# Product 4 of the first weight pair goes to the second level; gates get near due times; some splits write three quarters of a tile

## The chip, the cores and the metric

The kernel runs on one core of a Trainium2 chip. The metric is the device time of one execution in microseconds. The engines are TensorE (PE, with its weight loads as PEld), VectorE (DVE), ScalarE (ACT), GpSimd (POOL) and SyncE (SP). SP and POOL issue nearly all DMAs here. Each engine works through its own instructions in the order in which the program lists them.

## The reference

All values are float32, with one batch of 2048 positions, a width of 512 and a hidden width of 1792.

```python
xn = _layernorm(x)                                        # x: 2048 x 512
a, b = xn @ dft_hid_re.T, xn @ dft_hid_im.T
y = dft_seq_re @ a - dft_seq_im @ b                       # 2048 x 512
h = gelu(xn @ w_gate) * (xn @ w_up)                       # 2048 x 1792
out = x + y + h @ w_down
```

## The kernel before

**Precision.** Each float32 operand of a matmul is split into a high part, which ACT rounds (`split_hi`), and a low part, which DVE makes as source minus high part (`split_lo`). A product of two such operands is three matmuls: high by high, high by low and low by high (`mm3`, line 305 issues them all).

**Seven products in place of eight.** Every matrix product is cut into 2 x 2 blocks and computed with seven block products after Strassen and Winograd, numbered 0 to 6. The sums of blocks that these need are made by DVE. In the feed-forward part a *unit* n is one column block of the gate and up weights for one half of the positions: units 0 to 13 (NP = 14) are the first half of the positions (`sp` 0), units 14 to 27 use the same weights on the second half (`sp` 1). Even units are gates, odd units are ups. A unit's product is six matmuls of 128 x 512.

**The second level.** For two of the seven products, 0 and 4, the product of a weight pair (units n and n+1, n even) with both halves of the positions is again a product of 2 x 2 blocks. Plainly it is four unit products (n, n+1, n+14, n+15) of six matmuls each, 24 in all. The second level makes it as seven inner products of three matmuls each, 21 in all. `LEAD[r]` is the first unit from which product r does so: `LEAD = {0: 0, 4: 2}` means from unit 0 for product 0, and from unit 2 for product 4. The inner products are called Xrk in the order strings (line 1727): X46 is inner product 6 of product 4. "Y43" in an odd unit's string is X43 of the pair that began a unit earlier. All seven run in the first half of the positions. What they yield for units n+14 and n+15 is written to DRAM (`park_m`, line 1606) and fetched back much later (`load_m`, line 1549), where ACT copies it into a PSUM bank as the start of that unit's sum (`seed`, line 1638).

What the inner products of product r need:

- sums of position blocks of both halves, `inner_x` (line 688, four of them, `xi` in the profile), each followed by a split on ACT and DVE. They may not begin before unit `LEAD[r] - INNER_AHEAD`, INNER_AHEAD being 2. For r = 4 they use the block sums that `sum_x` (line 1467, DVE line 1473) makes for the second half of the positions.
- sums of weight blocks of both units, `inner_w` (line 699, four instructions of 128 x 128 on DVE, `wi` in the profile), and one split.
- three ACT copies between PSUM banks or to SBUF (`copy`, line 1593) and two DVE additions (`sums`, line 1602).

The weights' own splits (`weight_split`, line 645) make two products' operands with one instruction on ACT and one on DVE: k = 0 makes those of products 0 and 1, k = 1 those of 4 and 5, each 128 x 512 elements (2 blocks of 256 columns). From units 14 on, where product 0 or 4 comes from the second level, only half of it is split (`half_split`).

**The planner.** The order of every instruction is made by `Plan` before the kernel is built. An operation has an engine, a cost, what it waits for, how many of the 109 SBUF tiles it takes (`SLOTS`), and a due time. `deadlines` (line 73) lays the PE operations end to end, gives each its start as due time, and works back from there to everything that feeds it. Operations that nothing waits for get a due time near the end of the plan; those that empty a PSUM bank get their matmul's end plus 4 us. `choose` (line 115) takes, engine by engine, what can start first, and keeps an operation that takes tiles from starting earlier than `early` us ahead of its due time, and a load from starting earlier than `ahead` us before its own. There are two plans: the first covers the layer norm, the plain part and half of the sequence DFT, up to about 200 us; the second covers the rest.

**The second plan's stages.** The sequence DFT goes on in 32 steps (`step_ops`, line 1024). A step loads panels of the DFT matrix, sums some (DVE), splits them (ACT and DVE), and multiplies. Sixteen steps make a chunk, in two halves of eight; between the halves DVE works through a chain of eight additions from PSUM (lines 1071 to 1081), and products of the second half wait for its end. Meanwhile `x_norm` (line 1397) normalizes the transposed input tile by tile: SP loads one of 16 tiles (`xr<-in_xt`), DVE subtracts and multiplies (lines 610 and 611), POOL stores it to DRAM (line 1405), and SP fetches it back for the feed-forward part (`xr<-xnt`, line 606). Then the hidden DFT products (`y`) and the units follow. The down products (`dn`) and the last `y` products are put into the gaps of the units' order strings (d0 to d3). `hidden` (line 1700) makes the gate (ACT) and its product with the up unit (DVE) out of PSUM banks.

Of the kernel before, what the change touches and what calls it, by code (L numbers as in the profile page):

```python
# [14 lines left out]
P = 128  # L15
# [24 lines left out]
class Plan:  # L40
# [15 lines left out]
    def done(self, name, at):  # L56
        self.ends[name] = at

    def add(self, name, engine, cost, fn, after=(), makes=(), uses=(), due=None, mb=0, banks=(), holds=(), adds=False, begin=0., ahead=None):
        assert name not in self.ops, name  # L60
        after = list(after)
        if engine == "p":
            if self.products:
                after.append(self.products)
            self.products = name
        self.ops[name] = dict(e=engine, cost=cost, fn=fn, after=after, makes=dict(makes), due=due, mb=mb, adds=adds, begin=begin, ahead=ahead or self.ahead, early=self.early, banks=tuple(banks), drains=bool(holds) and engine != "p")
        self.size.update(makes)
        for k in (*dict(makes), *uses):
            self.users.setdefault(k, set()).add(name)
        for k in (*banks, *holds):  # L70
            self.held.setdefault(k, set()).add(name)

    def deadlines(self):
        then = {n: [] for n in self.ops}
        for n, o in self.ops.items():
            for a in o["after"]:
                if a in self.ops:
                    then[a].append(n)
        t = self.clock["p"]
        for o in self.ops.values():  # L80
            if o["e"] == "p":
                o["due"], t = t, t + o["cost"]
        late = self.LATE if self.early == self.LATE else t - 1
        order, seen = [], set()

        def visit(n):
            stack = [(n, iter(then[n]))]
            seen.add(n)
            while stack:
                m, it = stack[-1]  # L90
                for c in it:
                    if c not in seen:
                        seen.add(c)
                        stack.append((c, iter(then[c])))
                        break
                else:
                    stack.pop()
                    order.append(m)
        for n in self.ops:
            if n not in seen:  # L100
                visit(n)
        for n in order:
            o = self.ops[n]
            own = late if o["due"] is None else o["due"]
            if o["due"] is None and o["drains"]:
                own = max([self.ops[a]["due"] + self.ops[a]["cost"] for a in o["after"] if a in self.ops and self.ops[a]["e"] == "p"],
                          default=late) + 4
            took = o["cost"] + (3.5 + o["mb"] * 2.6 if o["mb"] else 0)
            tail = self.TAIL[o["e"]]
            o["due"] = min([own] + [self.ops[c]["due"] - took - tail * (self.ops[c]["e"] != "p" or o["e"] != "p") for c in then[n]])  # L110
# [145 lines left out]
def fnet_geglu_kernel(ctx: ExitStack, tc: tile.TileContext, x, xt, cs, dh, wgu, wd, out):  # L256
# [34 lines left out]
    def split_lo(t, src, sign=1, engine=nc.vector):  # L291
        hi = t[0].bitcast(F32)
        if sign > 0:
            engine.tensor_sub(t[1], src, hi)  # L294
        else:
            engine.scalar_tensor_tensor(t[1], src, -1.0, hi, op0=OP.mult, op1=OP.subtract)
# [324 lines left out]
    wx, wl = {}, {}  # L621
# [7 lines left out]
    def weight_sums(n):  # L629
# [3 lines left out]
        def put(k, h, op, u, v):  # L633
# [3 lines left out]
            if (k, h) == (1, 1):  # L637
# [4 lines left out]
                lambda: put(1, 0, OP.subtract, a[:, 0], b[:, 1]),  # L642
                lambda: put(1, 1, OP.subtract, a[:, 1], r[0][:, 1]))

    def weight_split(n, k):

        if k == 0 and short(n):
            v = slot("wh", F32R, (P, 2, HD)), slot("wl", F32R, (P, 2, HD))
            wl[n, 1], wl[n, 3] = ((v[0][:, i], v[1][:, i]) for i in range(2))
            return v, wx[n][0]  # L650
        if half_split(n, k):
            p, src = {3: (3, wx[n][3][:, 0]), 0: (1, wx[n][0][:, 1]), 1: (5, wx[n][1][:, 1])}[k]
            wl[n, p] = hl_half("w")
            return wl[n, p], src
        v = slot("wh", F32R, (P, 2, HD)), slot("wl", F32R, (P, 2, HD))
        for r, p in enumerate(((0, 1), (4, 5), (6, 2))[k]):
            wl[n, p] = v[0][:, r], v[1][:, r]
        return v, wx[n][k]

    def load_wd(q):  # L660
# [3 lines left out]
            for i in range(2):  # L664
                nc.sync.dma_start(wx["d", q][i].rearrange("p a b -> p (a b)"), wd[q % (NP // 2), i])

    LEAD = {0: 0, 4: 2}
    LATER = {0: False, 4: False}
    KEEP_SUMS = (10, NP)

# [269 lines left out]
    for k in range(2, L):  # L940
        n, m = seq[k]
# [358 lines left out]


    HURRY = 28
    LOOSE = 15
    STEP_EARLY = 12, 16
    LATER_HURRY = 28
    FETCH_AHEAD = 22
    W_AHEAD = 12
    TURNS = [[0], [1, 2], [3, 4], [5, 6], [7, 8, 9], [10, 11], [12, 13]]
    INNER_AHEAD = 2
    INTO_ACC = (6, 3)  # L1310
    SUMS_AT = 0
    U1 = 2 * NP
    PARK = [(0, 0), (4, 0), *((k, i) for k in (1, 5, 2) for i in range(2))]

# [12 lines left out]
        plan.size[key] = size  # L1327
        plan.had.add(key)

    def split_of(key, f, ready, uses, makes, wide=True, due=None, **kw):  # L1330

        def hi():
            begun[key] = f()
            split_hi(*begun[key])
        add(("hi", key), "a", A5 if wide else A2, hi, after=ready, uses=uses, makes=makes, **kw)
        add(("lo", key), "v", V5 if wide else V2, lambda: split_lo(*begun.pop(key)), after=[("hi", key)], uses=[*uses, *makes], due=due)

    def unit_at(n):
        return TU + n * 14.25
# [52 lines left out]
    plan.early, plan.ahead = HURRY, FETCH_AHEAD  # L1392
    y_ops((4, 2, 6), "z")

    NORM_AT, NORM_STEP = 10, 8

    def x_norm(sp, t, d):
        n = (sp * 2 + t) * ND + d
        at = T2 + NORM_AT + NORM_STEP * n
        if d == 0:  # L1400
            add(("xst", sp, t), "s", .9, lambda: load_st(sp, t), makes={("xst", sp, t): 2}, mb=2 * MB)
        raw, key = ("nr", sp, t, d), ("xr", sp, d, t)
        add(("nl", sp, t, d), "s", .45, lambda: load_xr(sp, t, d, xt[sp, t, d]), makes={raw: 1}, mb=MB)
        add(("nn", sp, t, d), "v", 2 * V5, lambda: norm_xT(sp, t, d), after=[("nl", sp, t, d), ("xst", sp, t)], uses=[raw, ("xst", sp, t)], due=at)
        add(("np", sp, t, d), "g", .6, lambda: nc.gpsimd.dma_start(xnt[sp, t, d], xr[sp, d, t]), after=[("nn", sp, t, d)], uses=[raw], mb=MB, due=at + 4)
        add(("xl", sp, d, t), "s", .45, lambda: load_xr(sp, t, d, xnt[sp, t, d]), after=[("np", sp, t, d)], makes={key: 1}, mb=MB)

    for sp in range(2):
        for t in range(2):
# [3 lines left out]
    def units():  # L1413

        def weights(m):
# [23 lines left out]
            for k in range(3 if short(m) else 4):  # L1439
                half = half_split(m, k)  # L1440
                split_of(("w", m, k), lambda k=k: weight_split(m, k), [("sw", m, 3)],
                         [("ws", m, k - 1)] if k in (1, 2) else [("wx", m)], {("wl", m, k): 1 if half else 2}, not half)
        def park_sums(m, at, d):
            for i in range(2):
                nc.gpsimd.dma_start(ws_park[d, at, i], wx[m][1 + i].rearrange("p a b -> p (a b)"))
# [16 lines left out]
        for q in range(NP):  # L1462
            weights(("d", q))

        X_UNIT = {0: 0, 4: 1.5, 1: 3, 5: 8, 2: 9, 6: 12, 3: 12}

        def sum_x(sp, i, k):
            b11, b12, b21, b22 = (xr[sp, d, t] for d in (i, 2 + i) for t in range(2))
# [10 lines left out]
        def x_ops(sp, i):  # L1479
# [9 lines left out]
            for k, src, ready in ((0, x[0], load[0]), (1, x[2], load[2]), (2, x[3], load[3]), (4, x[1], ("sx", sp, i, 1)), (5, x[4], ("sx", sp, i, 2)),  # L1489
# [9 lines left out]
                if name[0] == "xp":  # L1499
                    add(("px", k, i), "g", 1.2, lambda k=k: park_xT(k, i), after=[("lo", ("x", 1, k, i))], uses=[name], mb=2 * MB, due=unit_at(X_UNIT[k] + i / 2 + 1.3))  # L1500
                    add(("fx", k, i), "s", .9, lambda k=k: fetch_one(k, i), after=[("px", k, i)], makes={("xt", 1, k, i): 2}, mb=2 * MB)

        for sp in range(2):
            for i in range(2):
                x_ops(sp, i)
# [11 lines left out]

        for r in LEAD:
            (o0, o1), (n0, n1) = ([("xr", sp, i, r // 4) for i in range(2)] for sp in range(2))
            made = [("sx", sp, i, 1) if r else ("xl", sp, i, 0) for i in range(2) for sp in range(2)]  # L1520
            for k, after, uses in ((4, [], [n0, o0]), (6, [], [n0, n1]), (5, [("ix", r, 4)], [n1, ("ix", r, 4)]),
                                   (3, [("ix", r, 5)], [o1, ("ix", r, 5)])):
                add(("ix", r, k), "v", V5, lambda r=r, k=k: inner_x(r, k), after=after + made, uses=uses, makes={("ix", r, k): 1},
                    begin=unit_at(LEAD[r] - INNER_AHEAD))
                split_of(("i", r, k), lambda r=r, k=k: inner_xsplit(r, k), [("ix", r, k)], [("ix", r, k)], {("ixt", r, k): 2},
                         begin=unit_at(LEAD[r] - INNER_AHEAD))

        def inner_ready(n, r, k):
            if k in (0, 1):
# [170 lines left out]
        def hidden(n, blk, ready, src, holds, uses):  # L1700

            q, s = n // 2, ("s", n // 2, blk)
            if n % 2 == 0:
                add(("f", n, blk), "a", A5, lambda: gate(n, blk, src()), after=ready, makes={s: 1}, holds=holds, uses=uses)
                return
            add(("f", n, blk), "v", V5, lambda: up_1(n, blk, src()), after=[*ready, ("f", n - 1, blk)], holds=holds, uses=[*uses, s])
            if blk in H_USE:
                r = H_USE[blk]
                add(("hi", ("h", q, r)), "a", A5, lambda: up_2(n, blk), after=[("f", n, blk)], uses=[s], makes={("hl", q, r): 2})
                add(("lo", ("h", q, r)), "v", V5, lambda: up_3(n, blk), after=[("hi", ("h", q, r))], uses=[s, ("hl", q, r)])  # L1710
# [209 lines left out]
```

## Time and profile before

| | |
|---|---|
| time, median of 3 runs | 788.95 us |
| the runs | 787.11, 788.95 and 789.32 us |
| the profiled execution's own time | 788.03 us |
| its span, first to last instruction | 786.2 us |

The profile comes from one further execution. Its span leaves out 1.8 us of that execution's time, which lies around the first and last instruction. The page lists busy time by engine, the chain of work that ended last, and groups of instructions by source line; views of the trace list single instructions with their starts, and busy time in stretches. PE's busy time overlaps from one matmul to the next, so for PE the distance between starts tells more than the busy share. The units run from 380.5 us on, and the last matmul starts at 782.6 us.

### The profile page before, as it was taken

To read this page: it belongs to the slowest core of one execution; us is meant where nothing else is said; L and a number is where in the kernel's file an instruction comes from. 1 tells how busy PE (TensorE), PEld (TensorE's weight loads), DVE (VectorE), ACT (ScalarE), POOL (GpSimd) and SP (SyncE) were. 2 spreads that over 40 slices of the span, in tenths; PEclk is the share of its full clock that TensorE was granted. 3 is DMA by queue.
4 is the path that set the end of the run, shared out by engine and by line. 5 is a ranking of instruction groups with operands and counts; after the bars stand their busy time and mean duration, and the time that the engine had idled before them with its cause. 6 is when DMAs were issued, how large, how long until landed. Compare 5 with 4: busy or idle time off the path is not lost.

```text
span 786.2 us, 11771 instructions
## 1 busy us (share of the span) xinstructions
PE 781.9 (99%) x3444; PEld 644.5 (82%) x3444; DVE 741.1 (94%) x1408; ACT 553.1 (70%) x1050; POOL 176.7 (22%) x266
## 2 busy tenths in 40 slices
PE   9999999999999999999999999999999999999998
PEld 6888888888887888888888888888888888888886
DVE  7999999999899699998999996999999989999986
ACT  6997555556545274556867876778797789788864
POOL 0120520043221041000122432343322112222200
PEclk9999999999999999999999999999999999999999
DMA  9966998779999879992745995797899975999942
GB/s 329 388 182 204 350 350 275 247 272 279 362 371 368 294 268 365 394 374 87 214 162 138 200 214 129 127 297 175 206 296 329 254 197 90 268 324 259 243 111 108
DMA packets 102928, 198.47 MB, mean 252 GB/s; under 512 B 12208, under 2 KB 21456, under 8 KB 102672
## 3 DMA queue, kind: packets, MB, share of 16 engines
q1 hardware_dynamic: 75312, 129.29, 47.1%
q0 software_dynamic: 27264, 68.17, 35.8%
q8 instruction: 27, 0.44, 0.2%
q14 instruction: 37, 0.30, 0.1%
q10 hardware_dynamic: 288, 0.26, 0.1%
HBM read 126.62 MB, written 74.20 MB: 255 GB/s over the span
## 4 chain that ended last, share of the span: by engine, by line
PE 99%; DMA 1%; DVE 0%; issue 0%
PE m L305 35%; PE b L305 20%; PE dn L305 17%; PE y L305 10%; PE c L305 8%; PE a L305 5%; PE z L305 4%; DMA xr<-in_xt 1%; PE warm L794 1%; DVE m L1081 0%; PE warm L796 0%; DVE p L1837 0%; PE st L1232 0%; DVE c L1079 0%
## 5 line engine op out<-in xcount | busy, mean ns | idle before, releaser
L289 ACT ACTIVATE psh<-pan 128x512 fp32r<-128x512 f32 x203 | 118.1, 626 | 77.5 <-DVE pan L581 26.2
L294 DVE TENSOR_TENSOR psl<-pan,psh 128x512 fp32r<-128x512 f32 x198 | 129.3, 685 | 0.1
L1686 POOL DMA_DIRECT2D partial<-part x80 | 70.0, 881 | 191.2 <-ACT part L1683 159.4
L305 PE MATMUL m<-psh,xch 128*128 128x512 f32 x232 | 90.4, 389 | 0.1
L305 PE MATMUL m<-psh,xcl 128*128 128x512 f32 x232 | 90.3, 389 | 0.0
L305 PE MATMUL m<-psl,xch 128*128 128x512 f32 x232 | 90.3, 389 | 0.0
L1683 ACT ACTIVATE part<-dn 128x512 f32<-128x512 f32 x80 | 47.1, 592 | 20.9 <-PE dn L305 16.7
L305 PEld LDWEIGHTS m<-psh,xch 128*128 128x128 f32 x232 | 43.5, 188 | 9.6 <-DVE m L1081 0.5
L305 PEld LDWEIGHTS m<-psl,xch 128*128 128x128 f32 x232 | 43.5, 188 | 9.0
L305 PEld LDWEIGHTS m<-psh,xcl 128*128 128x128 f32 x232 | 43.6, 188 | 9.0
L294 DVE TENSOR_TENSOR wl<-ws,wh 128x512 fp32r<-128x512 f32 x72 | 48.5, 685 | 1.6 <-ACT wh L289 1.6
L289 ACT ACTIVATE wh<-ws 128x512 fp32r<-128x512 f32 x72 | 43.6, 626 | 1.5 <-DMA partial<-part 1.2
L581 DVE TENSOR_TENSOR pan<-pan 128x512 f32<-128x512 f32 x58 | 39.1, 684 | 2.3 <-PE m L305 2.2
L305 PE MATMUL m<-psh,xa 128*128 128x512 f32 x116 | 40.4, 389 | 0.0
L546 POOL DMA_DIRECT2D partial<-part x28 | 20.8, 770 | 86.9 <-ACT part L542 73.2
L1046 POOL DMA_DIRECT2D t_park<-pan x29 | 16.5, 568 | 100.0 <-DVE pan L582 91.4
L289 ACT ACTIVATE hth<-s 128x512 fp32r<-128x512 f32 x56 | 34.1, 627 | 5.5 <-DVE s L753 5.3
L294 DVE TENSOR_TENSOR htl<-s,hth 128x512 fp32r<-128x512 f32 x56 | 37.3, 685 | 0.1
L753 DVE TENSOR_TENSOR s<-s 128x512 f32<-128x512 f32 x56 | 37.3, 685 | 0.1
L1599 ACT ACTIVATE q<-b 128x512 f32<-128x512 f32 x41 | 24.4, 596 | 14.4 <-PE b L305 14.1
L1599 ACT ACTIVATE w<-b 128x512 f32<-128x512 f32 x41 | 24.5, 597 | 13.9 <-PE b L305 11.2
L305 PE MATMUL dn<-htl,wh 128*128 128x512 f32 x84 | 32.7, 389 | 0.0
(760 smaller groups left out, 2419.4 us busy)
## 6 DMA issues: line engine op xcount, KB each, us to landing
pan<-in_cs SPq DMA_DIRECT2D x157, 256.0 KB, 6.5
partial<-part POOLq DMA_DIRECT2D x108, 256.0 KB, 5.2
wx<-in_wgu SPq DMA_DIRECT2D x48, 256.0 KB, 5.1
t_park<-pan POOLq DMA_DIRECT2D x29, 256.0 KB, 5.7
pan<-t_park SPq DMA_DIRECT2D x29, 256.0 KB, 6.0
wd<-in_wd SPq DMA_DIRECT2D x28, 256.0 KB, 5.5
acc<-partial SPq DMA_DIRECT2D x28, 256.0 KB, 4.7
m<-m_park SPq DMA_DIRECT2D x26, 256.0 KB, 6.0
```

Source lines behind the costliest of these rows:

```text
L289: nc.scalar.activation(t[0], src, AF.Copy, scale=float(sign))
L294: engine.tensor_sub(t[1], src, hi)
L305: nc.tensor.matmul(ps, a[u][:, sl], b[v], start=first and r == 0, stop=last and r == 2, skip_group_check=resumed)
L546: nc.gpsimd.dma_start(partial[sp, r, j], ypart.pop((r, j)), **({} if r in (0, 5, 6) else {"accum_op": OP.add}))
L581: return [lambda: nc.vector.tensor_sub(t3, b22, b12), lambda: nc.vector.tensor_sub(t1, b12, b11), lambda: (nc.vector.tensor_sub(b22, *((t1 ...
L753: nc.vector.tensor_sub(t, u, v)
L794: nc.tensor.matmul(ps, ones[:, :P], ones, start=i == 0, stop=False)
L1046: plan.add(("park", i), "g", .6, lambda: nc.gpsimd.dma_start(t2_park[c, k], pan_src[i][5]), after=[("S", i, 2)], mb=MB, uses=[("r", i, b22)])
L1599: nc.scalar.activation((bank if banks else side)[(n, to, *more)], src(), AF.Copy)
L1683: nc.scalar.activation(part[0], tiles[j], AF.Copy)
L1686: add(("da", qs[-1], r, j), "g", .6, lambda j=j, part=part: nc.gpsimd.dma_start(partial[sp, r, j], part[0], accum_op=OP.add), after=[("dc" ...
```

## The change

- `LEAD[4]` goes from 2 to 0, so that product 4 of units 0, 1, 14 and 15 is made by X40 to X46 in units 0 and 1. The order strings follow from it: unit 0 takes the first string below in place of the second, unit 1 the third in place of the fourth, and units 14 and 15 lose their product 4.
- `weight_split` leaves out the first 128 of the 512 columns in odd units of the first half of the positions where the product comes from the second level (`trimmed`): that quarter holds the half of product 0's (or 4's) operand that no inner product reads by itself (X03 and X43 read the other half). The planner's costs of these splits fall by 0.11 and 0.13 us.
- The planner gets `soon`: an operation that has it is due at the latest so many microseconds after it can be ready. Gates and their products with the up units have `SOON` = 5.
- Due times and limits move. Steps' tiles may be made 16 us ahead (12 before) and their loads 20 us ahead (16 before). The block sums and splits of the positions may be made 50 us ahead (28 before), and the normalized tiles fetched back 45 us ahead (22 before). Normalized tiles are due every 7 us (8 before). The second half's block sums begin one unit earlier, and its split for product 4 begins at unit 0.5 (1.5 before).

The order strings of `order`, lines 1729, 1731, 1733 and 1735, unchanged themselves:

```python
"X00 X40 d1 X01 X41 X04 5 1 X05 d2 6 X06 X44 d0 3 X03 X02 X45 2 d3 X46"    # lead(n, 4)
"X00 4 X01 d1 5 1 d2 X04 6 X05 d0 3 X06 d3 2 X03"                          # lead(n, 0) alone
"5 Y43 1 d1 Y42 d2 6 d0 3 d3 2"                                            # lead(n - 1, 4)
"4 Y02 d1 5 1 d2 6 d0 3 d3 2"                                              # lead(n - 1, 0) alone
```

```diff
     def deadlines(self):
...
+        ready = {}
+        for n in reversed(order):
+            o = self.ops[n]
+            ready[n] = o["due"] if o["e"] == "p" else max([ready[a] + self.ops[a]["cost"] for a in o["after"] if a in self.ops], default=0.)
         for n in order:
...
+            if o["soon"] is not None:
+                own = min(own, ready[n] + o["cost"] + o["soon"])
...
+    def trimmed(n, k):
+        return isinstance(n, int) and k < 2 and lead(n - 1, 4 * k)
+
     def weight_split(n, k):
...
+        if trimmed(n, k):
+            v, src = ([t.rearrange("p a b -> p (a b)")[:, P:] for t in u] for u in (v, (wx[n][k],)))
+            return v, src[0]
         return v, wx[n][k]
...
-    LEAD = {0: 0, 4: 2}
+    LEAD = {0: 0, 4: 0}
...
+    X_EARLY, X_FETCH = 50, 45
+    SOON = 5
     LOOSE = 15
-    STEP_EARLY = 12, 16
+    STEP_EARLY = 16, 20
...
-    SUMS_AT = 0
+    SUMS_AT = -1
...
-        add(("hi", key), "a", A5 if wide else A2, hi, after=ready, uses=uses, makes=makes, **kw)
-        add(("lo", key), "v", V5 if wide else V2, lambda: split_lo(*begun.pop(key)), after=[("hi", key)], uses=[*uses, *makes], due=due)
+        add(("hi", key), "a", (A5 if wide else A2) - .11 * less, hi, after=ready, uses=uses, makes=makes, **kw)
+        add(("lo", key), "v", (V5 if wide else V2) - .13 * less, lambda: split_lo(*begun.pop(key)), after=[("hi", key)], uses=[*uses, *makes], due=due)
...
-    NORM_AT, NORM_STEP = 10, 8
+    NORM_AT, NORM_STEP = 10, 7
...
-        add(("xl", sp, d, t), "s", .45, lambda: load_xr(sp, t, d, xnt[sp, t, d]), after=[("np", sp, t, d)], makes={key: 1}, mb=MB)
+        add(("xl", sp, d, t), "s", .45, lambda: load_xr(sp, t, d, xnt[sp, t, d]), after=[("np", sp, t, d)], makes={key: 1}, mb=MB, ahead=X_FETCH)
...
-        X_UNIT = {0: 0, 4: 1.5, 1: 3, 5: 8, 2: 9, 6: 12, 3: 12}
+        X_UNIT = {0: 0, 4: 0.5, 1: 3, 5: 8, 2: 9, 6: 12, 3: 12}
...
+        plan.early = X_EARLY
         for sp in range(2):
             for i in range(2):
                 x_ops(sp, i)
...
+        plan.early = HURRY
...
-                add(("f", n, blk), "a", A5, lambda: gate(n, blk, src()), after=ready, makes={s: 1}, holds=holds, uses=uses)
+                add(("f", n, blk), "a", A5, lambda: gate(n, blk, src()), after=ready, makes={s: 1}, holds=holds, uses=uses, soon=SOON)
                 return
-            add(("f", n, blk), "v", V5, lambda: up_1(n, blk, src()), after=[*ready, ("f", n - 1, blk)], holds=holds, uses=[*uses, s])
+            add(("f", n, blk), "v", V5, lambda: up_1(n, blk, src()), after=[*ready, ("f", n - 1, blk)], holds=holds, uses=[*uses, s], soon=SOON)
```

More of the change, by code (lines that the diff above doesn't have):

```diff
@@ L57, in done, with add @@
         self.ends[name] = at
-    def add(self, name, engine, cost, fn, after=(), makes=(), uses=(), due=None, mb=0, banks=(), holds=(), adds=False, begin=0., ahead=None):
+    def add(self, name, engine, cost, fn, after=(), makes=(), uses=(), due=None, mb=0, banks=(), holds=(), adds=False, begin=0., ahead=None, soon=None):
         assert name not in self.ops, name
@@ L65, in add @@
             self.products = name
-        self.ops[name] = dict(e=engine, cost=cost, fn=fn, after=after, makes=dict(makes), due=due, mb=mb, adds=adds, begin=begin, ahead=ahead or self.ahead, early=self.early, banks=tuple(banks), drains=bool(holds) and engine != "p")
+        self.ops[name] = dict(e=engine, cost=cost, fn=fn, after=after, makes=dict(makes), due=due, mb=mb, adds=adds, begin=begin, soon=soon, ahead=ahead or self.ahead, early=self.early, banks=tuple(banks), drains=bool(holds) and engine != "p")
         self.size.update(makes)
@@ L1328, in have, with split_of @@
         plan.had.add(key)
-    def split_of(key, f, ready, uses, makes, wide=True, due=None, **kw):
+    def split_of(key, f, ready, uses, makes, wide=True, due=None, less=False, **kw):
         def hi():
@@ L1441, in weights @@
                 split_of(("w", m, k), lambda k=k: weight_split(m, k), [("sw", m, 3)],
-                         [("ws", m, k - 1)] if k in (1, 2) else [("wx", m)], {("wl", m, k): 1 if half else 2}, not half)
+                         [("ws", m, k - 1)] if k in (1, 2) else [("wx", m)], {("wl", m, k): 1 if half else 2}, not half,
+                         less=trimmed(m, k))
         def park_sums(m, at, d):
```

## The prediction

> **What bounds the kernel now.** I read the page first: the span, the busy times, the clock row and the chain.
>
> ```profile
> span 786.2 us, 11771 instructions
> PE 781.9 (99%) x3444; PEld 644.5 (82%) x3444; DVE 741.1 (94%) x1408; ACT 553.1 (70%) x1050; POOL 176.7 (22%) x266
> PEclk9999999999999999999999999999999999999999
> PE 99%; DMA 1%; DVE 0%; issue 0%
> ```
>
> PE carries the chain at the full clock, and DVE has 6% to spare. A busy share can hide idle time, since matmuls overlap, so I went on to the chain in order of time and the starts of single matmuls.
>
> ```profile
> 96.98 76.16 PE m L305 x336
> ```
>
> These 336 matmuls in 76.16 us are one every 0.2267 us. That is the price of a matmul for as long as nothing keeps PE waiting. Going through all starts, I found three gaps that exceed it by over 0.15 us once the products have begun:
>
> ```profile
> 244.83 0.39 PE L305 MATMUL m<-psh,xf11l 128*128 128x512 f32 x1
> 245.29 0.50 PE L305 MATMUL m<-psh,xf11h 128*128 128x512 f32 x1
> ...
> 246.56 0.40 PE L305 MATMUL m<-psh,xf11l 128*128 128x512 f32 x1
> 247.05 0.49 PE L305 MATMUL m<-psh,xch 128*128 128x512 f32 x1
> ```
> ```profile
> 464.58 0.39 PE L305 MATMUL dn<-htl,w 128*128 128x512 f32 x1
> 464.98 0.50 PE L305 MATMUL b<-xT30h,w 128*128 128x512 f32 x1
> 465.31 0.39 PE L305 MATMUL b<-xT30l,w 128*128 128x512 f32 x1
> ```
>
> Each stall is the distance less 0.227, and the start after it is late too (0.33 for 0.227, as the last pair shows). The first two are 0.23 and 0.27 plus about 0.11 each, so 0.7 us; the third is 0.17 + 0.10, so 0.3 us. **All stalls together are about 1.0 us.** The kernel can be helped in two ways alone: fewer matmuls, or this 1.0 us. The Trainium skill, Perfetto Trace Analysis, Identifying the Most-Contended Engine, speaks against the first: it calls matmul busy time no good measure and takes the busy share of LDWEIGHTS. By that share, 82% on the page, TensorE has slack, and the sum would be 0 for the matmuls in place of the -0.68 below; the starts above do not bear that out.
>
> **The matmuls.** Product 4 of units 0, 1, 14 and 15 was 4 x 6 = 24 matmuls and becomes 7 x 3 = 21: three fewer, 3 x 0.2267 = **-0.68 us**. This is the only certain term. They move too: the first pair gets 21 - 12 = 9 more (+2.04 us), units 14 and 15 get 12 fewer (-2.72 us).
>
> **DVE, over the whole run.** Prices are distances between starts, since a busy DVE overlaps its instructions:
>
> ```profile
> 395.47 0.42 DVE L636 TENSOR_TENSOR ws<-wx 128x256 f32<-128x256 f32 x1
> 395.81 0.42 DVE L294 TENSOR_TENSOR w<-wx,w 128x256 fp32r<-128x256 f32 x1
> ...
> 402.76 0.28 DVE L707 TENSOR_TENSOR wi<-wi,wx 128x128 f32<-128x128 f32 x1
> 402.96 0.28 DVE L707 TENSOR_TENSOR wi<-wx 128x128 f32<-128x128 f32 x1
> ...
> 425.25 0.68 DVE L294 TENSOR_TENSOR xT41l<-xr,xT41h 128x512 fp32r<-128x512 f32 x1
> 425.86 0.68 DVE L294 TENSOR_TENSOR xi43l<-xi,xi43h 128x512 fp32r<-128x512 f32 x1
> ```
>
> 128 columns cost 0.20, 256 cost 0.34 and 512 cost 0.61 us. No row has 384 columns; the bounds are 0.34 and 0.61, and I take the middle, 0.47, because the three lie on a line. The new pair adds 4 x 0.20 (`inner_w`), one split and two `sums` at 0.61: 2.6 us. The half splits in units 14 and 15 save 2 x 0.27 and the 14 trimmed ones (seven odd units, k = 0 and 1) 14 x 0.14: 2.5 us. DVE's total stays. ACT gains three copies, a split and two seeds, six at about 17.12/35 = 0.5 us each (the stretch below, ACT's busy time over its count), and has 30% idle. Two stores on POOL and two loads on SP of 256 KB are added; POOL is 78% idle, and the seeds that wait for the loads are needed for product 2, late in a unit. I price all of this at nothing; if a seed's load came late, PE would stand for up to the 6.0 us such a load takes:
>
> ```profile
> m<-m_park SPq DMA_DIRECT2D x26, 256.0 KB, 6.0
> 580.00:600.00 20.00, 20.00 (x90) 16.53 (x89) 19.96 (x41) 17.12 (x35) 5.78 (x8) 1.00 1.04 335
> ```
>
> The DMA engines are full there (1.04, the number before the last), but 26 such loads already run from there on without a stall, each asked for up to 22 us ahead by the planner.
>
> **DVE, where it matters: units 0 and 1.** What product 4 needs is not new, it is early. This is PE's first matmul of unit 0:
>
> ```profile
> 380.46 0.39 PE L305 MATMUL a<-xT00h,wh 128*128 128x512 f32 x1
> ```
>
> In the new string X44 stands behind 45 matmuls (X00 3, X40 3, d1 6, X01, X41, X04 9, 5 and 1 12, X05 3, 6 6, X06 3), so it is due at 380.46 + 45 x 0.2267 = 390.7; X45 behind 66 at 395.4, X46 behind 75 at 397.5, X43 behind 84 at 399.5. Before, the same work stood here:
>
> ```profile
> 357.45 0.42 DVE L636 TENSOR_TENSOR ws<-ws,wx 128x256 f32<-128x256 f32 x1
> 361.62 1.33 DVE L1177 TENSOR_TENSOR zr<-c,zr 128x512 f32<-128x512 f32 x2 [3.75 <-ACT c L1145]
> ...
> 394.27 0.69 DVE L1603 TENSOR_TENSOR w<-c,w 128x512 f32<-128x512 f32 x1 [0.34 <-ACT w L1599]
> ...
> 397.42 0.69 DVE L1195 TENSOR_TENSOR zr<-zr 128x512 f32<-128x512 f32 x1
> ...
> 398.95 0.68 DVE L1603 TENSOR_TENSOR q<-c,q 128x512 f32<-128x512 f32 x1
> ...
> 408.08 0.69 DVE L1473 TENSOR_TENSOR t<-xr 128x512 f32<-128x512 f32 x1
> ...
> 412.56 0.69 DVE L693 TENSOR_TENSOR xi<-xr 128x512 f32<-128x512 f32 x1
> ```
>
> The four block sums of the second half (from 408.08), four `xi` sums (from 412.56) and their four low splits (the last at 425.86 above) are 12 x 0.61 = 7.3 us; with `inner_w` and its split, 1.4, **8.7 us must be in by 399.5** that were not. Cover: the idle 3.75 and 0.34 us in these rows, together 4.1; work of 395 to 399 that nobody needs yet (four 128x256 sums of unit 2's weights, two `zr`, a parked `q`: 4 x 0.34 + 3 x 0.61 = 3.2); two trimmed splits, 0.3. That is 7.6, and 1.1 us has to go earlier than 350. There is a hole for it:
>
> ```profile
> 260.00:270.00 10.00, 10.00 (x46) 8.29 (x45) 7.88 (x13) 3.15 (x7) 1.08 (x2) 1.00 0.96 328
> 270.00:280.00 10.00, 10.00 (x46) 8.29 (x45) 5.47 (x9) 5.86 (x12) 1.59 (x3) 1.00 0.48 185
> ...
> 330.00:340.00 10.00, 10.00 (x46) 8.28 (x45) 10.00 (x18) 5.57 (x11) 0.00 (x0) 1.00 1.05 388
> ...
> 350.00:360.00 10.00, 10.00 (x46) 8.29 (x45) 7.87 (x14) 6.21 (x11) 0.00 (x0) 1.00 0.37 138
> 360.00:370.00 10.00, 10.00 (x45) 8.28 (x45) 8.32 (x14) 6.24 (x11) 0.00 (x0) 1.00 0.33 107
> ```
>
> DVE (fourth number) leaves 2.1 + 4.5 us at 260 to 280. Steps' tiles may now be made 16 us ahead instead of 12, and the normalizing ends about 15 us sooner, so more than 1.1 us can slip back into it. I take the stall in unit 0 or 1 at zero, with bounds of -0.3 (the stall at 464.58 may go) and +4.9 (second rival).
>
> **Loads.** X44 needs the block sums by about 386, so four tiles fetched late must come sooner:
>
> ```profile
> xr<-xnt SPq DMA_DIRECT2D x16, 256.0 KB, 5.4
> SPq L556 <- PE m L305: 10.5, 2, 9.6
> ```
> ```profile
> 349.34 0.96 SPq L627 DMA_DIRECT2D wx<-in_wgu  x2
> 360.25 1.46 SPq L556 DMA_DIRECT2D zr<-z_park  x2
> ...
> 373.47 1.47 SPq L606 DMA_DIRECT2D xr<-xnt  x2
> ...
> 377.95 1.21 SPq L606 DMA_DIRECT2D xr<-xnt  x2
> ```
>
> Issued at 373 and 378 and landing 5.4 us later (first row), they would just do; with 45 us of allowance they go into SP's queue ahead of weights, `zr` and `dh`. SP stands still from 350 to 360, mostly until PE's last steps free tiles (9.6 us, second row), and the DMA share is 0.37 and 0.33 from 350 to 370: the four fit by bandwidth, if they find tiles. Normalizing closer together (7 for 8 us, from 208 on)
>
> ```profile
> L610 DVE TENSOR_TENSOR xr<-xr,bst x16: 682/685/694, 208.4 to 324.5; 128x512 f32<-128x512 f32 x16
> ```
>
> puts (250 - 208)/7 - (250 - 208)/8 = 0.75 tile more, two transfers of 256 KB each, in front of 250, where the engines are full (rival three).
>
> **Gates.** `soon` adds no instruction; it moves gates ahead of splits. ACT has idle time; on DVE, one up product put in front of an operand that is just in time costs at most 0.61 us once. I take zero.
>
> **The sum.** 788.03 - 0.68 = 787.35 us for an execution like the profiled one. The median of the runs is 0.92 above that execution, which gives 788.27 by it. I take a value between: **787.7 us**. A measurement of this kernel tells about 0.3%, 2.4 us, from no change, and the runs before spread over 2.2.
>
> **The rivals.**
>
> 1. *The stalls go as well.* The chain of additions at 245 gets a new order on DVE. For it: DVE gets ahead earlier. Against: it is as full there as before. 788.03 - 0.68 - 1.0 = 786.35 (787.3 by the median). Chance 0.2.
> 2. *Slower: DVE is late for X44 to X43.* The hole at 357 to 361 is a wait in DVE's queue, with SP short of tiles at the same time; if the second half's tiles find no room before the steps end at 364, neither this hole nor the one at 260 takes any of the 8.7 us. Then 8.7 - 0.34 - 3.2 - 0.3 = 4.9 us are missing, and PE stands behind X44 with every product of the unit queued after it: 788.03 - 0.68 + 4.9 = 792.2. It makes the kernel slower by over 0.3% once 3.1 us are missing. For it: DVE is at 10.00 of 10 from 330 on and PE's order is fixed. Against: units 2 and 3 ran the same strings before without a gap. Chance 0.11. The Trainium skill (Perfetto Trace Analysis, Per-engine timelines) says that ACT and DVE are strictly first in, first out; the 3.75 us row, with later work ready, agrees.
> 3. *A late load at 240 to 250.* 0.75 x 2 transfers of 256 KB at the 388 GB/s of a full stretch are 1.0 us, DVE waits in its queue, and the stall at 245 grows by it: 788.35 (789.3 by the median). Chance 0.16.
> 4. *PE has slack, so that the three matmuls were never paid for* (the change then moves no time): 788.03. The starts speak against it. Chance 0.03.
>
> **How the numbers follow.** The forecast keeps 0.5. Range: 785.9 (the first rival less half a microsecond of scatter) to 790.6 (the third by the median, with scatter, or half of the second); most of the second lies outside. Faster by over 0.3% means below 786.6 against the median: about half of the first rival and a little of the forecast's scatter, 0.14. Slower: the second and little else, 0.12. Within: 0.74.
>
> **What would show it.** The profile after should have 3441 matmuls, the same distance between starts, `xi44l` before 390.7, and no start of PE between 380 and 400 that is late. A gap of PE at X44 to X43 with DVE behind it is the second rival, a longer one near 245 the third. I am wrong by more than the range if the new order of the second plan stalls in a stage that I have priced at zero.

## The result, and the profile after

| | before | changed |
|---|---|---|
| time, median of 13 runs each, side by side | 788.82 us | 790.12 us |
| lowest and highest | 787.11, 789.36 | 789.31, 791.85 |
| profiled execution | 788.03 | 790.12 |
| its span | 786.2 | 788.3 |

The ratio is 1.0024, with a 95% interval of 1.0016 to 1.0032. The time lies inside the predicted range and within 0.3%, but on the other side: 1.1 us less were forecast, 1.3 us more came out.

From the page of the changed kernel, the span, the busy times, the granted clock and the chain by engine:

```profile
span 788.3 us, 11776 instructions
...
PE 780.9 (99%) x3441; PEld 643.8 (82%) x3441; DVE 743.2 (94%) x1415; ACT 555.5 (70%) x1056; POOL 177.6 (23%) x268
...
PEclk9999999999999999999999999999999999999999
...
PE 88%; issue 5%; DMA 2%; DVE 2%; POOL 2%; ACT 1%; POOLq 0%; DVEq 0%; ACTq 0%
```

The clock is full and three matmuls are gone, as meant; DVE's 94% is as before. What differs is the chain: PE carried 99% of it and carries 88% now. Other engines let PE wait somewhere, and the busy shares don't say where. So I listed every start of PE once more. This is PE's timeline of the changed kernel (start, duration, operation, and in brackets the idle time before it with what ended it) at each distance that is too long, and at two matmuls that the prediction named:

```profile
389.10 0.39 PE L311 MATMUL b<-xT61h,wl 128*128 128x512 f32 x1
389.70 0.50 PE L311 MATMUL b<-xi06h,wih 128*128 128x512 f32 x1 [0.21 <-ACT q L1617]
...
390.50 0.40 PE L311 MATMUL c<-xi44h,wih 128*128 128x512 f32 x1
...
399.35 0.39 PE L311 MATMUL b<-xi43h,wh 128*128 128x512 f32 x1
...
412.72 0.39 PE L311 MATMUL c<-xT41h,wl 128*128 128x512 f32 x1
414.04 0.50 PE L311 MATMUL c<-xi04h,wih 128*128 128x512 f32 x1 [0.93 <-DVE s L752]
...
467.82 0.39 PE L311 MATMUL dn<-htl,w 128*128 128x512 f32 x1
469.08 0.50 PE L311 MATMUL b<-xT30h,w 128*128 128x512 f32 x1 [0.88 <-ACT w L1617]
...
526.80 0.39 PE L311 MATMUL b<-xT51h,wl 128*128 128x512 f32 x1
527.38 0.50 PE L311 MATMUL b<-xi43h,wh 128*128 128x512 f32 x1 [0.20 <-ACT w L1617]
```

Less the usual 0.227, and with 0.11 each for the late start behind it, there are four stalls: **A** at 389 (0.48 us), **B** at 412 (1.20), **C** at 467 (1.15, where before lost 0.3) and **D** at 527 (0.47). The two near 245 are gone. The whole run, from the starts of the matmuls:

| us, profiled executions | before | changed | difference |
|---|---|---|---|
| first product starts | 5.25 | 5.41 | +0.16 |
| stalls (distances over 0.235, less 0.227 each) | 1.40 | 3.74 | +2.34 |
| all the rest up to the last matmul's start | 775.97 | 775.37 | -0.60 |
| last matmul starts | 782.62 | 784.52 | +1.90 |

The three matmuls brought their 0.6 to 0.7 us, and stalls took 2.3. None of them stands at X44 to X43, where the prediction had looked for one: X44 ran at 390.50 and X43 at 399.35, without a wait. But A, at X06 just ahead of X44, is a late start between 380 and 400, one of its signs, and C stands at the same pair of matmuls as the stall of 0.3 us at 464.58 that it had listed.

**Stall A.** First ACT's timeline of the changed kernel, with the places of C and D for later, then that of before, and from PE's timeline of before X06 and, for stall B, X04:

```profile
386.62 0.62 ACT L295 ACTIVATE xT01h<-xr 128x512 fp32r<-128x512 f32 x1
387.26 1.28 ACT L747 ACT_TABLE_LOAD   x1
388.56 0.60 ACT L747 ACTIVATE s<-a 128x512 f32<-128x512 f32 x1
389.05 0.59 ACT L1617 ACTIVATE q<-b 128x512 f32<-128x512 f32 x1
...
466.94 0.63 ACT L295 ACTIVATE hh<-s 128x512 fp32r<-128x512 f32 x1 [1.84 <-DVE s L752]
467.48 1.06 ACT L1701 ACTIVATE part<-dn 128x512 f32<-128x512 f32 x2
468.43 0.60 ACT L1617 ACTIVATE w<-b 128x512 f32<-128x512 f32 x1
...
526.73 0.60 ACT L1617 ACTIVATE w<-b 128x512 f32<-128x512 f32 x1 [0.45 <-DMA partial<-part]
```
```profile
386.72 1.28 ACT L735 ACT_TABLE_LOAD   x1
388.01 0.60 ACT L735 ACTIVATE s<-a 128x512 f32<-128x512 f32 x1
...
390.18 0.60 ACT L1599 ACTIVATE q<-b 128x512 f32<-128x512 f32 x1
```
```profile
392.70 0.39 PE L305 MATMUL b<-xi06h,wih 128*128 128x512 f32 x1
...
411.06 0.39 PE L305 MATMUL c<-xi04h,wih 128*128 128x512 f32 x1
```

X06 adds to the bank in which X05's sum stands, and the copy `q<-b` has to read that sum out first. X06 starts when this copy ends, at 389.64. That copy stands behind the first gate, and the first gate brings the load of the GELU table along, 1.28 us in which ACT does nothing else. In before the same load began 0.5 us sooner, at 386.72, but X06 came at 392.70, 1.9 us after its copy had ended (390.18 + 0.60). In the new string X06 is due at 389.33, 3.4 us sooner, and the load has become the thing that it waits for.

**Stall B.** DVE's timeline of the changed kernel, with rows for other steps, and that of before:

```profile
384.35 0.69 DVE L300 TENSOR_TENSOR xi44l<-xi,xi44h 128x512 fp32r<-128x512 f32 x1
...
389.50 0.56 DVE L300 TENSOR_TENSOR wl<-wx,wh 128x384 fp32r<-128x384 f32 x1
389.97 0.69 DVE L300 TENSOR_TENSOR xT01l<-xr,xT01h 128x512 fp32r<-128x512 f32 x1
...
397.30 0.69 DVE L300 TENSOR_TENSOR xi43l<-xi,xi43h 128x512 fp32r<-128x512 f32 x1
...
411.77 0.68 DVE L300 TENSOR_TENSOR z310l<-zr,z310h 128x512 fp32r<-128x512 f32 x1
412.37 0.68 DVE L300 TENSOR_TENSOR z311l<-zr,z311h 128x512 fp32r<-128x512 f32 x1
412.97 0.42 DVE L642 TENSOR_TENSOR ws<-ws,wx 128x256 f32<-128x256 f32 x1
413.31 0.68 DVE L752 TENSOR_TENSOR s<-s,b 128x512 f32<-128x512 f32 x1
...
460.87 0.43 DVE L642 TENSOR_TENSOR ws<-wd 128x256 f32<-128x256 f32 x1 [2.27 <-DMA wd<-in_wd]
```
```profile
406.54 0.69 DVE L294 TENSOR_TENSOR z310l<-zr,z310h 128x512 fp32r<-128x512 f32 x1
...
409.62 0.68 DVE L740 TENSOR_TENSOR s<-s,b 128x512 f32<-128x512 f32 x1
```

X04 of the second pair opens a PSUM bank that this up product (`s<-s,b`) has to leave first. In before the up product began at 409.62 and X04 ran at 411.06 without a wait. Now it begins at 413.31, behind two splits and a weight sum for later matmuls. It ends at 413.99, and PE starts at 414.04. The same three stood ahead of it in before, but there the first of them began at 406.54, 5.2 us sooner (411.77 now): DVE's queue as a whole comes later to this place, and PE's X04 only 1.9 us later.

**Stalls C and D.** At C DVE stands 2.27 us for a `wd` load (460.87), ACT then stands 1.84 us for DVE (466.94), and the copy `w<-b` that frees PE's bank follows only at 468.43, behind two copies of down products. At D the copy waits for a tile that a store still reads. These are chains of several engines; A and B each hang on the place of one instruction, as the runs below show.

### The profile page after: what moved, and what is told of

Read it like the earlier page. It is cut to its first block, busy times and chain, and to the rows that moved or that the text cites. A ratio compares the mean times of both kernels' runs of the same rounds, so it can differ in the third digit from the quotient of the medians.

```text
span 788.3 us, 11776 instructions
## 1 busy us (share of the span) xinstructions
PE 780.9 (99%) x3441; PEld 643.8 (82%) x3441; DVE 743.2 (94%) x1415; ACT 555.5 (70%) x1056; POOL 177.6 (23%) x268
## 4 chain that ended last, share of the span: by engine, by line
PE 88%; issue 5%; DMA 2%; DVE 2%; POOL 2%; ACT 1%; POOLq 0%; DVEq 0%; ACTq 0%
PE m L311 35%; PE b L311 15%; PE dn L311 15%; PE y L311 9%; PE c L311 5%; PE z L311 4%; PE a L311 4%; POOL partial L1704 1%; DMA partial<-part 1%; DMA wd<-in_wd 1%; POOL m_park L1625 0%; DMA x<-in_x 0%; DVE ws L642 0%; DVE wl L300 0%; POOL xT_hl L625 0%
## 5 line engine op out<-in xcount | busy, mean ns | idle before, releaser
L300 DVE TENSOR_TENSOR wl<-ws,wh 128x512 fp32r<-128x512 f32 (+1 forms) x70 | 46.4, 672 | 2.1 <-ACT wh L295 2.0
L295 ACT ACTIVATE wh<-ws 128x512 fp32r<-128x512 f32 (+1 forms) x70 | 42.4, 616 | 1.7 <-DVE ws L642 1.3
L311 PE MATMUL dn<-hth,wh 128*128 128x512 f32 x84 | 32.7, 389 | 0.0
```

The lines of the kernel that those rows point to most:

```text
L295: nc.scalar.activation(t[0], src, AF.Copy, scale=float(sign))
L311: nc.tensor.matmul(ps, a[u][:, sl], b[v], start=first and r == 0, stop=last and r == 2, skip_group_check=resumed)
```

## The experiments

The theory: stalls A and B come of two instructions that stand too late in the queues of ACT and DVE, and neither engine is short of time. The first rival: DVE is full, so an operation moved ahead there makes another one late. The second: the loss lies with the later stalls, whatever happens in units 0 to 3. All edits start from the changed kernel. "Stalls" are worked out from the profiled execution as in the table above; they are given with the late start behind them. Each group of runs has before in it, so kernels of different groups compare best by their ratios to before. The closer normalizing of the tiles and the earlier block sums were not undone singly.

**The changed kernel again**, no edit:

> The changed kernel once more, for a second trace. Two theories stand. Theory 'order': the 2.3 us that the stalls grew by come from single instructions that stand in the wrong place in an engine's order; then the stalls that follow from the order alone, 0.6 us at 389 and 1.3 us at 412.7, stand in this trace again to within 0.1 us, while those at 468 (1.3 us) and 527 (0.6 us), which followed a late transfer or a tile that came free late, may differ by up to 1 us. Time 790.1, give or take 0.6. Rival 'shortage': DVE has too much to do from 350 us on, so that the lost time moves about; the first two stalls shift by several us or change size.

790.48 us, ratio to before (788.49 in this group) 1.0026 [1.0017, 1.0035]. The stalls stood at 389.08, 412.70, 467.78 and 526.79, within 0.04 us of the first profile; A, B and C have the same size within 0.04 us, D is 0.70 for 0.47. They belong to the program, not to one execution.

**The table load earlier.** One GELU of a scratch column between the two plans, where ACT waits anyway:

```diff
     first_half = plan
+    nc.scalar.activation(junk[:, :1], eps, AF.Gelu_apprx_tanh)
```

> One gate function on 128x1 elements is added on ACT between the two plans, at about 200 us, so that the table load of 1.28 us, which stands at 387.3 us right ahead of the first gate, happens there. Theory 'order': the copy that X06 waits for is no longer behind the table load, and the stall at 389 (0.48 us and 0.11 us after it) goes; the stall at 412.7 stays at 1.3. Time 0.6 below the changed kernel, 789.5. Rival 'shortage': X06 finds its operands late from DVE as well, and the stall stays or moves to the next inner product; 790.1.

789.71 us, 1.0014 [1.0005, 1.0023]: 0.8 us below the changed kernel. ACT's timeline shows the load in its new place, and none follows up to the first gate:

```profile
201.77 1.28 ACT L1330 ACT_TABLE_LOAD   x1
203.06 0.21 ACT L1330 ACTIVATE junk<-eps 128x1 bf16<-128x1 f32 x1
```

Stall A is gone and B is unchanged (1.10 + 0.11 at 412.62). C fell to 0.28 and D to 0.32, though every engine's order is otherwise that of the changed kernel: a shift in time is enough. (The profiled execution, 788.86, was this kernel's fastest.) The Trainium skill, ScalarE: Activation LUTs, What ACT_TABLE_LOAD costs, gives 1283 ns for the load and 1380 ns for a drain with it, 2.66 us for a switch. The load's 1.28 us agrees. The drain does not show: in the changed kernel the split before the load starts at 386.62 and the gate behind it at 388.56, 1.94 us from start to start with the load inside.

**The up products sooner.** The two up products of unit 1 that hold a bank get a nearer due time:

```diff
-  ... holds=holds, uses=[*uses, s], soon=SOON)
+  ... holds=holds, uses=[*uses, s], soon=2 if holds and n == 1 else SOON)
```

> Only the two up products of unit 1 that read a PSUM bank get a due time, 2 us after they can be ready, where they had 4 us after their matmuls on a clock that runs late. No work is added or left out. Theory 'order': their banks come free before X04 of the second pair asks for one, the stall of 1.3 us at 412.7 goes and nothing takes its place; time 1.3 below the changed kernel, 788.8, a little less if the later stalls shift. Rival 'shortage': DVE's order only changes who is late; a stall of about 1.2 us shows up at another product between 400 and 430 us, and the time stays at 790.1.

788.03 us, 0.9995 [0.9986, 1.0004]: 2.4 us below the changed kernel, about twice what was expected. Stall B is gone and nothing took its place on DVE, which speaks against the first rival. A stayed (0.37 + 0.11 at 388.90). The second half of the gain came from later: C fell from 1.19 to 0.34 and D from 0.70 to nothing. So the later stalls are not the fixed loss that the second rival takes them for. Up to X04 of stall B the edit moved these two products alone in DVE's order; behind it the planner made another order (380 of DVE's 1415 places differ), so whether C and D fell because B went or because of that later order is not told apart.

**Product 4 of the first pair as before**, all other parts kept:

```diff
-    LEAD = {0: 0, 4: 0}
+    LEAD = {0: 0, 4: 2}
```

> Of the change, LEAD alone is undone: product 4 of the first pair is plain again, and every due time, limit and trimmed split of the change stays. Three matmuls come back, +0.68 us. Theory 'order': the stalls at 389 and 412.7, which belong to the first pair's new strings, are gone (-1.9); 788.9 if the later stalls (1.9 us) stay as they are, 787.0 if they go too. Rival, that the moved due times themselves cost the time: it stays at or above 790.

789.60 us, 1.0014 [1.0005, 1.0022]. The expectation was missed. A and B went, as they had to if the new string makes them, but new stalls came at 607.71 (2.11), 686.00 (0.33) and 725.81 (0.63). ACT's and PE's timelines at the largest:

```profile
607.98 0.63 ACT L295 ACTIVATE hth<-s 128x512 fp32r<-128x512 f32 x1 [3.24 <-issue]
...
609.30 0.59 ACT L1617 ACTIVATE w<-b 128x512 f32<-128x512 f32 x1
```
```profile
607.71 0.39 PE L311 MATMUL dn<-hl,wh 128*128 128x512 f32 x1
609.94 0.50 PE L311 MATMUL b<-xT30h,w 128*128 128x512 f32 x1 [1.84 <-ACT w L1617]
```

It is the pattern of C: a split of the hidden values stands at the head of ACT's queue after 3.24 us without work (DVE finishes its source `s` at 607.90, 0.08 us ahead of it), and the copy that frees PE's bank waits behind it. With the other parts of the change alone the kernel is slower, too.

**Both moves together**:

> The gate's table load early and the two up products of unit 1 due sooner, together. Theory 'order': the stalls at 389 and 412.7 are both gone, the one near 467 is 0.3 to 0.5; the two gains add, and the time is 788.03 (up products sooner alone) less 0.6, so 787.4, some 1.0 below the kernel before. Rival 'shortage': with both holes closed DVE is late elsewhere between 380 and 430, and the time stays at 788.

786.72 us (786.45 to 787.31), 0.9981 [0.9972, 0.9989]: **faster than both kernels**, 1.7 us (0.2%) below before and 3.4 to 3.8 below the changed kernel, about 3.5 by the ratios. In the three timelines (ACT, PE and DVE) the gate no longer brings a load, the copy runs 0.95 us sooner, and neither X06 nor X04 waits:

```profile
387.42 0.60 ACT L747 ACTIVATE s<-a 128x512 f32<-128x512 f32 x1 [0.24 <-PE a L311]
388.10 0.60 ACT L1618 ACTIVATE q<-b 128x512 f32<-128x512 f32 x1
```
```profile
389.04 0.39 PE L311 MATMUL b<-xT61h,wl 128*128 128x512 f32 x1
389.26 0.39 PE L311 MATMUL b<-xi06h,wih 128*128 128x512 f32 x1
...
412.16 0.39 PE L311 MATMUL c<-xT41h,wl 128*128 128x512 f32 x1
412.38 0.39 PE L311 MATMUL c<-xi04h,wih 128*128 128x512 f32 x1
```
```profile
410.99 0.68 DVE L752 TENSOR_TENSOR s<-s,b 128x512 f32<-128x512 f32 x1
```

One stall of over 0.1 us is left after the first 20 us: 0.34, at 465.88.

**And the last stall filled.** Unit 5's string puts d2 behind product 6, where it stood ahead of it, so that six down-product matmuls in place of three stand between products 6 and 3:

```diff
+            if n == 5:
+                return "5 Y43 1 d1 Y42 6 d2 d0 3 d3 2"
```

> As both_moved, and in unit 5 the filler d2 stands behind product 6 instead of ahead of it, so that six matmuls instead of three stand between product 6 and product 3, which waits for ACT's copy of product 6. Theory 'order': the stall near 467 (0.23 us and 0.11 after it) goes as well; no stall is left between 380 us and the end, and the time is 0.35 below both_moved. Rival: the copy is late because ACT waits for DVE, not for want of matmuls, and the stall stays at 0.2 or more.

787.20 us, 0.9988 [0.9979, 0.9997], a miss: the stall is gone, and the time is no better than without the edit. The profiled execution was this kernel's slowest (789.19) and has stalls at 707.41, 711.61 and 723.83 (0.77, 0.62 and 1.07). Whether the typical execution has them can't be said from it.

**The position sums as late as before:**

```diff
-    X_EARLY, X_FETCH = 50, 45
+    X_EARLY, X_FETCH = 28, 22
```

> Of the change, X_EARLY and X_FETCH alone are undone: the positions' block sums and splits may again be made 28 us ahead and the normalized tiles fetched 22 us ahead. This puts the prediction's second rival to the test: DVE cannot have what X44 to X43 need in time. By that rival's sum PE stands for up to 4.9 us between X04 of the first pair and the end of unit 1, and the time is 790.1 + 4.9 = 795 with the changed kernel's other stalls. If DVE has room after 350 us anyway, PE stands no longer than in the changed kernel: 790.1.

796.86 us, 1.0111 [1.0097, 1.0125]. PE's timeline:

```profile
384.53 0.39 PE L311 MATMUL c<-xT41h,wl 128*128 128x512 f32 x1
386.64 0.50 PE L311 MATMUL c<-xi04h,wih 128*128 128x512 f32 x1 [1.73 <-DVE zr L1204]
...
398.24 0.50 PE L311 MATMUL b<-xi45l,wih 128*128 128x512 f32 x1 [0.17 <-DVE xi45l L300]
...
399.96 0.39 PE L311 MATMUL c<-xT21h,wl 128*128 128x512 f32 x1
400.71 0.50 PE L311 MATMUL b<-xi46h,wih 128*128 128x512 f32 x1 [0.36 <-ACT xi46h L295]
401.72 0.50 PE L311 MATMUL b<-xi46l,wih 128*128 128x512 f32 x1 [0.51 <-DVE xi46l L300]
```

This is the prediction's second rival, at the place that it named (X45 and X46 wait for `xi45l`, `xi46h` and `xi46l`), some 2 us, and 2.0 us stand at X04 besides, which waits until DVE's `zr<-m,zr` of the last DFT steps has ended: a bank again, and not an operand. The execution's stalls add up to 12.1 us; only some 4 of them lie between 384 and 403, the others follow in later units.

**The splits untrimmed, at the same order:**

```diff
-        if trimmed(n, k):
+        if False:
```

> The trimmed splits write all 512 columns again, and nothing else changes: the planner still counts them as short, so every engine's order is that of the changed kernel. Each of 28 instructions is longer, by 0.14 us on DVE and 0.1 us on ACT. If DVE is what PE waits for at 412.7 us, the splits of unit 1 that stand ahead (two on DVE, 0.27 us) make that stall 0.3 longer, and the time is 790.4 to 790.8; if the trimming is off the path it stays at 790.2.

790.75 us, 1.003 [1.0019, 1.0041], against 1.0026 for the changed kernel: not told apart. The time lies where the expectation put a trim on the path, but the mechanism is not there: B should have grown by 0.3 us and is unchanged to 0.01. In this profile the later stalls are larger (0.68 at 464.18, which is new, and 0.93 for D). So at B the trim lies off the path; whether it is worth something in later units is not shown.

**One accumulating store left out**, to see whether it holds the tile that the `wd` load of stall C waits for:

```diff
- lambda j=j, part=part: nc.gpsimd.dma_start(partial[sp, r, j], part[0], accum_op=OP.add)
+ lambda j=j, part=part: None if (qs[0], r, j) == (0, 5, 0) else nc.gpsimd.dma_start(partial[sp, r, j], part[0], accum_op=OP.add)
```

> One accumulating store of the first down product (turn 0, product 5, column block 0) is left out of the changed kernel, in an unchanged order, so that its share is missing from the output. In the trace of the changed kernel it was issued at 447.9 us and SP waited until 453.9 for the tile that it held, before it could load the down weights that DVE then missed for 2.3 us. Theory 'late tile': the load goes out at 447 to 448, DVE's wait at 458.6 goes, and the stall at 467.8 falls from 1.3 us (with what follows it) to about 0.3; the time is 0.9 below the changed kernel, 789.3. Rival, that the copy for product 3 is late by ACT's own order: the stall stays at 1.1 or more, 790.2.

790.27 us, 1.003 [1.0019, 1.0042]: a miss. SP still waited 5.6 us at that load, again for a `partial<-part` store, so it was not this store that held the tile. C did fall to 0.28, but D grew to 0.96, and three small stalls came at 710 to 726. C goes with DVE's wait for the `wd` load: in four profiles that wait is 1.97 to 2.65 us and C is 0.97 to 1.19; here it is 1.02, with the early table load 1.20, and C is 0.28 both times. Why the load lands late in some orders, and what sets D, is not settled.

**Both moves, product 4 of the first pair as before** (`LEAD = {0: 0, 4: 2}` with the two edits):

> both_moved with LEAD undone: product 4 of the first pair is plain again, every other edit stays. The three matmuls are worth 0.68 us by the distance of starts, so the time is 786.72 + 0.68 = 787.4 if no new stall comes with the order; by the theory 'order' any amount above that must stand in the trace as a stall of PE at one place after 450 us, 1 to 3 us, as in lead_undone. If the second level itself cost time (more DVE and ACT work), it would be faster than both_moved.

788.99 us, 1.0015 [1.0006, 1.0023] (before 788.16). That is 2.3 us above both moves, and three matmuls are 0.7 of them. Its profiled execution has 2.85 us of stalls where that of both moves has 0.70: 0.28 at 246.18, the rest at 464.11, 607.98, 685.22 and 724.89 (0.33, 1.05, 0.21 and 0.64). So the remainder is stalls late in the run again, and not another price of the matmuls.

**Both moves, `soon` undone elsewhere** (`SOON = None`; the two up products keep their 2):

> both_moved without the near due times of gates and up products that read no PSUM bank (SOON undone); the two up products of unit 1 and the early table load stay. The prediction priced SOON at zero. If that holds: 786.7, or up to 1 us more or less by a stall that comes or goes with the new order after 420 us. If near due times are what keeps the later units free of stalls, several stalls of 0.5 us and over stand there, and the time is above 788.

786.84 us, 0.9984 [0.9976, 0.9993]. With both moves in place, `soon` as the change has it is worth nothing; a nearer due time for two instructions alone is worth 2.4 us in the changed kernel.

**The steps' tiles as late as before:**

```diff
-    STEP_EARLY = 16, 20
+    STEP_EARLY = 12, 16
```

> The changed kernel with STEP_EARLY undone alone (steps' tiles 12 us ahead, loads 16). The kernel before lost 0.7 us at 245 to 247 in two stalls, the changed kernel none. Theory: the larger allowance took them away, and they come back: 790.2 + 0.7 = 790.9. Rival: the closer normalizing did, which brought DVE ahead; no stall there, and 790.2. The stalls at 389 and 412.7 stay at 0.6 and 1.3.

789.42 us, 1.0017 [1.0008, 1.0026]; the theory had it above the changed kernel. No stall came back at 245, so the closer normalizing, or another part, removed those, not the steps' wider limit. A and D went, B and C stayed.

**All executions together.** Taking the stalls and the first product's start away from the last matmul's start leaves this:

| kernels | matmuls | what is left, us |
|---|---|---|
| before, lead_undone, both_moved_lead_undone | 3444 | 775.97, 776.01, 776.03 |
| the eleven with product 4 from unit 0 | 3441 | 775.24 to 775.48 |

14 of the matmuls (`warm`) run before the first product; the other 3430 or 3427, 0.2263 us each, make these figures. So in every kernel the time from the first product to the last matmul is the count of these matmuls, 0.2263 us each, plus the stalls. Between the two rows lie 0.5 to 0.8 us for three matmuls.

## Why the prediction was wrong

- **PE bounds, a matmul costs 0.2267 us, three fewer are worth 0.68 us**: right. Rival 4 (PE has slack) falls by the last table, and with it the busy share of weight loads, still 82% in the changed kernel, as a measure of what can be saved here.
- **DVE and the 384 columns**: the total stayed nearly (743.2 for 741.1 us busy), and the split cost what was estimated: from 389.50 to 389.97 is 0.47 us.
- **DVE where it matters, X44 to X43**: right at the places named. `xi44l` was made at 384.35 for 390.50, `xi43l` at 397.30 for 399.35. The experiment with late sums shows that the second rival is a real mechanism and that the wider limits keep it away.
- **Loads, rival 3**: no late load at 240 to 250; both stalls there went, 0.7 us, which the forecast had left standing.
- **Gates**: zero for `soon` was right in the sum (786.84 without it and 786.72 with it, both moves in place), but the risk was looked for on the wrong side. I asked what an up product put in front of an operand would cost; what cost was an up product put behind operands.
- **The step that failed** is "I take the stall in unit 0 or 1 at zero". I followed what the new inner products need and asked nothing of the banks that they need. X06 came 3.4 us sooner, and a table load lay in front of the copy that has to read its bank first (0.48 us, in unit 0). The up product of unit 1 came 3.7 us later, while the next pair's X04, which needs its bank, was due only 1.9 us later (1.20 us, in unit 2). The two edits that move these instructions took 3.4 to 3.8 us off and ended at 786.72: A and B are 1.7 of it, and most of the rest is C and D, which are smaller or gone in the order that the second edit made. 786.72 lies between the first rival's two figures, 786.35 for an execution like the profiled one and 787.3 by the median. The value zero could be had, but not with this order.
- **No term for later units**: "I price all of this at nothing" was said of the copies, seeds, stores and loads that the new pair adds. C's growth of 0.85 us and D's 0.47 lie in units 5 and 9, whose products the change leaves as they were, and the sum has nothing for them; only the prediction's last sentence names a stage priced at zero that stalls. Most of the experiments show that such stalls come and go with the order. The early table load, which left every order as it was, shows that a shift in time is enough. Why one order has them and another has not is read from the traces (a copy in ACT's queue behind a split that waits for DVE, a load that waits for a tile), and was not settled by a run.

## What to carry to other kernels

When an operation is moved sooner on the engine that bounds, list for it not only its operands but whoever must leave its PSUM bank, and what stands ahead of that instruction in its own queue: a table load or a few splits are enough. When a change of order loses a microsecond though its mechanism holds, take the distances between matmul starts, find the one instruction behind each late one, and move that alone. In this planned order, with the bounding engine at 99%, nearly every edit changed the stalls after 430 us, mostly by 0.5 to 2.2 us and once by 4, so a part of a change can be judged only with the rest in place.

## What was not expected of the hardware

- In two profiled executions of the changed kernel the stalls stand within 0.04 us of the same places, and three of four have the same size to 0.04. Over all 14 profiles the first product starts anywhere between 5.0 and 5.4 us. In two of them 0.5 to 0.9 us more was lost in the first 12 us (at 6.7 or 6.9, and at 11).
- One load of the GELU table serves the whole run: with the early load the trace shows no further one, though more than 180 copies and roundings run on ACT between it and the first gate.
- A single profiled execution can mislead by 2 us: the kernel with the filled stall was profiled at 789.19 and has a median of 787.20.
